# Attention, an ELU layer and a Mish layer on one core: states loaded first on two queues, identity from an iota, four slices and one output weight moved to split form, and new engine times in the plan

## The chip, the cores and the metric

One core of a Trainium2 chip runs the whole program. The metric is the device time of one execution in microseconds (us); lower is better. TensorE (PE) multiplies, VectorE (DVE) and ScalarE (ACT) do the elementwise work, GpSimd (POOL) a few memsets and reductions, and SyncE (SP) issues most of the transfers.

## What is computed

Inputs are float32. `x` is (4, 8, 512, 64), `state` is (4, 8, 32, 64), and each of the two feed-forward layers has `w_in` (512, 2048) and `w_out` (2048, 512). Cut from the reference:

```python
scores = scale * x @ state.T            # tokens read the state
xread  = softmax(scores) @ state        # (4, 8, 512, 64)
scores2 = scale * state @ x.T           # the state reads the tokens
sread  = softmax(scores2) @ x           # (4, 8, 32, 64)
y = concat([xread, sread], axis=2)      # -> (2176, 512) token rows
h = y @ moe_w_in;  y = elu(h) @ moe_w_out
h = y @ moe2_w_in; y = (h * tanh(softplus(h))) @ moe2_w_out
```

In the kernel the weights arrive as 64-bit words and are turned into float32 on the chip, by ScalarE and VectorE.

## The kernel before

**A plan sets every order.** The program first collects operations in a `Plan`: each has one engine or a choice of two (`EITHER`: ScalarE or VectorE), a cost in us, what it reads and writes, and a due time, either given or worked backwards from its successors (`dues`). `run` is a list scheduler: it takes for each engine the operation that can begin first (then the one due first) and emits instructions in that order. On the chip each engine runs its list strictly in order and waits for semaphores; so the costs in the plan affect nothing but orders and the choice between ScalarE and VectorE. The queues SP and ACTQ (transfers issued by ScalarE) are planned with an issue time, a rate and a latency.

**The start.** `load_states(0, 1)` brings the state of batch 0 in two transfers, `load_states(1, B)` the others. `states` transposes them on PE with the identity (L418) and copies them into the block layout `sd`. `front(b, hf)` loads x of batch b, head half hf, in two transfers (`load_x`, L560), transposes it (xT, L681) and multiplies by `sd` into scores (L692); `back` does the softmax on VectorE and ScalarE (L714 to L726), transposes the result (pT, L731) and copies it to the first layer's operand `x1`. `make_ident` (L337 to L346) builds the identity on VectorE. `warm` runs 14 bf16 products on zeroes (L361) ahead of it all; their operand is the zeroed `sd[3]`.

**The first layer** is organised in steps (b, j) over 16 slices of 128 hidden units for each batch of 512 tokens, in the order `FIRST`: slices 0 to 7 of batch 0, 0 to 7 of batch 1, then 8 to 15 of each, then batches 2 and 3. The attention output is never formed: `fold` (L528) multiplies the state into the slice of `w_in` and gives `m`, and a step multiplies `m` by the softmax. `mm1` makes the hidden slice h, `hidden` applies the ELU, `mm2` of the step two back adds g times `w_out` into four accumulators.

**Two forms of a product.** In the split form each float32 operand is a sum of two fp32r parts (hi is a cast, lo a subtraction), and three fp32r products replace the float32 one: L850 to L852 in `mm1`, L950 to L952 in `mm2`. In the whole form the float32 operands go to PE directly: L836 in `mm1` for the steps in `WHOLE` (slices 0 to 7 of batch 0), L938 in `mm2` for the first `WHOLE_OUT` slices of batch 0. Each float32 product leaves two records in the trace. The split form needs more of VectorE and ScalarE: `fold_slice` (cast and L549) for the slice of `m`, `split_first` (cast and subtraction) once for the softmax of batch 0, `split_g` (L914, L915) for g, `split_weight` (cast and L496) for `w_out`.

**After the first layer's start** come the state reads (`state_reads`, `squares` for batches 2 and 3), the conversion of the second layer's weights into a DRAM buffer, four steps for the state rows, and the second layer in five token blocks (L850 to L852, L897 to L915, L950 to L952).

Of the kernel before, what the change touches and what calls it, by code (L numbers as in the profile page):

```python
# [53 lines left out]
class Op:  # L54
    __slots__ = ("engs", "cost", "fn", "preds", "succs", "bufs", "due", "n", "end", "lag", "seq")


class Plan:
# [59 lines left out]
    def run(self, take, dma):  # L118
# [18 lines left out]
        while todo:  # L137
            best = None
            for e, lst in ready.items():
                at = free.get(e, 0.0)  # L140
                cand, first = None, None
                for due, seq, t, op in lst:
                    if op.end is not None:
                        continue
                    ok = True
                    need = {}
                    for b in op.bufs:
                        if b.t is None:
# [12 lines left out]
                    k = (t, due, seq)  # L161
                    if cand is None or k < cand[0]:
# [33 lines left out]
            else:  # L196
                free[e] = op.end = t + c
# [19 lines left out]
def attention_elu_mish(  # L217
# [59 lines left out]
    def act(n):  # L277
        return 0.22 + 0.00075 * n

    def dve(n):  # L280
        return 0.16 + 0.00104 * n
# [53 lines left out]
    def make_ident():  # L335
        cols, rows = (pools["at"].tile([P, 32], F32, tag=n, bufs=1, name=f"ident_{n}") for n in ("col", "tot"))
        nc.vector.memset(cols[:, 0:1], 0.0)  # L337
        w = 1
        while w < 32:
            nc.vector.tensor_scalar(cols[:, w:2 * w], cols[:, 0:w], float(w), None, ALU.add)  # L340
            w *= 2
        nc.vector.transpose(rows, cols)
        nc.vector.memset(ident, 0.0)
        for a in range(4):
            r = slice(32 * a, 32 * (a + 1))
            nc.vector.tensor_tensor(ident[r, r], cols[r, :], rows[r, :], ALU.is_equal)  # L346

    add("DVE", 2.8, make_ident, w=["ident"], due=-50.0)
# [41 lines left out]
    def zero():  # L390
        return sd[B - 1].rearrange("p g h t n -> p (g h t n)")[:, 0:P].bitcast(mybir.dt.bfloat16)
# [5 lines left out]
    def load_states(b0, b1):  # L397
# [13 lines left out]
    def states(b0, b1, due=None):  # L411
# [8 lines left out]
        A("PE", 0.25 * (b1 - b0), turn, r=["ident", (raw, 0), (raw, 1)], w=[pt], due=due)  # L420
        for b in range(b0, b1):
            for i in range(2):
                r = slice(i * D, (i + 1) * D)
                A(EITHER, {"ACT": 0.41, "DVE": 0.43}, lambda e, b=b, i=i, r=r: copy(
# [12 lines left out]
    def weight(kind, layer, j, due=None):  # L437
# [24 lines left out]
        add("ACT", 0.68, lambda: nc.scalar.activation(y.t, words()[0].bitcast(F32), AF.Prelu, scale=2.0 ** -112,  # L462
                                                      alpha=2.0 ** 32), r=[raw], w=[y])

        add("DVE", 0.43, lambda: nc.vector.tensor_scalar(u32(y), u32(y), 3, None, ALU.logical_shift_left), r=[y], w=[y])
# [13 lines left out]
        add("DVE", 0.69, lambda: nc.vector.scalar_tensor_tensor(  # L479
# [12 lines left out]
    def split_weight(kind, layer, j, v):  # L492
        w = w_sb[kind, layer, j] = buf("w", f"w_{kind}", NF, [P, 2, DM], F32R, f"w_{kind}{layer}_{j}_")
        add(EITHER, {"ACT": 0.61, "DVE": 0.43}, lambda e: copy(e, w[:, 0, :], v.t), r=[v], w=[(w, 0)])
        lo, cost = (nc.gpsimd, {"POOL": 1.3}) if (kind, layer, j) in POOL_LO else (nc.vector, {"DVE": 0.69})
# [45 lines left out]
    def fold_slice(s):  # L541
# [6 lines left out]
        add(EITHER, {"ACT": 0.41, "DVE": 0.33}, lambda e: copy(e, t[:, 0], src()), r=keys, w=[(t, 0)])  # L548
        add("DVE", 0.43, lambda: nc.vector.tensor_tensor(t[:, 1], src(), t[:, 0].bitcast(F32), ALU.subtract),  # L549
# [5 lines left out]
    def load_x(b, hf, due=None):  # L555

        t = buf("at", "xb", XB, [P, HH, NC, D], F32, "xb")
        for q in range(2):
            h = hf + 4 * q
            A(SP, 256.0 * (W_WEIGHT if early else 1.0), lambda q=q, h=h: nc.sync.dma_start(  # L560
# [4 lines left out]
    def load_x_ones(b, hf):  # L565

        t = buf("at", "xb", XB, [P, NC, HH, D + 1], F32, "xb1_")
        A("POOL", 0.1, lambda: nc.gpsimd.memset(t[:, :, :, D:], 1.0), w=[(t, HH)])
        for h in range(HH):
# [3 lines left out]
              w=[(t, h)], lag=1.0)  # L573
        return t

    def squares(b):

        xq = []
        for q in range(2):
            t = buf("at", "xb", XB, [P, 2 * S], F32, "xq")  # L580
            xq.append(t)
            for u in range(2):
                for e in range(2):
# [3 lines left out]
                        out=t[r].rearrange("p (k i) -> p k i", i=NS), in_=src), w=[(t, u, e)], lag=1.0)  # L587
# [5 lines left out]
        pr = buf("at", "xb", XB, [P, 2 * S], F32, "prob")  # L593
# [13 lines left out]
        A("PE", TILED + 0.9, score, r=[*xq, ("sd", b, 0), ("sd", b, 1)], w=pts, lag=1.0, place=[raw])  # L607
# [18 lines left out]
        A("DVE", 0.19, lambda: nc.vector.tensor_scalar(mx.t, mx.t, EPS, None, ALU.add), r=[mx], w=[mx])  # L626
        A("DVE", 0.35, lambda: nc.vector.reciprocal(mx.t, mx.t), r=[mx], w=[mx])
# [15 lines left out]
    def front(b, hf):  # L643
# [31 lines left out]
        lag = 0.0 if early else 1.0  # L675
        for q in range(2):
# [8 lines left out]
            A("PE", NC * (0.11), turn, r=["ident", (xb, q)], w=[pt], lag=lag, place=[xT])  # L685
            A(EITHER, both(S), lambda e, q=q, pt=pt: copy(e, xT[:, q, :], pt.t), r=[pt], w=[(xT, q)])
        pt = bank("scores")
        for q in range(2):
            def score(q=q):
                for i in range(4):  # L690
# [5 lines left out]
            A("PE", 0.9, score, r=[(xT, q), ("sd", b, 0), ("sd", b, 1)], w=[(pt, q)], lag=lag, place=held)  # L696
        all_c = [(pt, q) for q in range(2)]
# [5 lines left out]
    def back(b, hf):  # L703
# [10 lines left out]
        A("DVE", 0.69, lambda: nc.vector.tensor_reduce(mx.t, pv(), AX.X, ALU.max), r=all_c, w=[mx])  # L714
        less = A("DVE", 0.69, lambda: nc.vector.tensor_tensor(prg(), pv(), wide(mx), ALU.subtract),
                 r=all_c + [mx], w=[kp])
        A("ACT", 0.64, lambda: nc.scalar.activation(pr(), pr(), AF.Exp, scale=SCALE), r=[kp], w=[kp], lag=lag)
# [5 lines left out]
        A("DVE", 0.69, lambda: nc.vector.tensor_reduce(sm.t, prg(), AX.X, ALU.add), r=[kp], w=[sm])  # L723
        A("DVE", 0.17, lambda: nc.vector.tensor_scalar(sm.t, sm.t, EPS, None, ALU.add), r=[sm], w=[sm])
        A("DVE", 0.25, lambda: nc.vector.reciprocal(sm.t, sm.t), r=[sm], w=[sm])
        A("DVE", 0.69, lambda: nc.vector.tensor_tensor(prg(), prg(), wide(sm), ALU.mult), r=[kp, sm], w=[kp])  # L726
# [15 lines left out]
    def state_reads(b, due):  # L742
        st = buf("at", "own", 1, [P, 2, D])
        den = buf("at", "den", 2, [P, 2])
        xbs, raws = [], []
        order = "(c p f) -> p c f" if b in SQUARES else "(p c f) -> p c f"
        for hf in range(2):
            xbs.append(load_x_ones(b, hf))
# [8 lines left out]
            A("DVE", 1.04, lambda raw=raw, col=col: nc.vector.tensor_reduce(  # L757
# [43 lines left out]
    def split_first():  # L801
# [4 lines left out]
        for hf in range(2):  # L806
            add(EITHER, {"ACT": act(S), "DVE": 0.43}, lambda e, hf=hf: copy(e, t[:, 0, hf, :], v[:, hf, :]),
                r=[(v, hf)], w=[(t, hf, 0)])
            add("DVE", 0.69, lambda hf=hf: nc.vector.tensor_tensor(
# [52 lines left out]
    def hidden(s, h):  # L862
# [3 lines left out]
        if kind < 2:  # L866
# [4 lines left out]
            add("ACT", act(n) + 0.12, lambda: nc.scalar.activation(E(), E(), AF.Relu, bias=one, scale=-1.0),  # L871
# [21 lines left out]
        for q, (c0, c1) in enumerate(g.parts):  # L893
# [4 lines left out]
            add("DVE", 0.1 + 0.00065 * n, lambda c=c: nc.vector.tensor_scalar(e[:, c], e[:, c], E20, None, ALU.min),  # L898
# [3 lines left out]
            add("ACT", act(n) + 0.12, lambda c=c: nc.scalar.activation(e[:, c], u[:, c], AF.Ln, bias=two),  # L902
                r=[ku, "two"], w=[ke])
            add("ACT", act(n) + 0.03, lambda c=c: nc.scalar.activation(e[:, c], e[:, c], AF.Exp, scale=-1.0),  # L904
# [56 lines left out]
    def retire(kind, blk, j, acc, s):  # L961
# [22 lines left out]
        for i, a in enumerate(acc):  # L984
# [29 lines left out]
    def load_x2(nb):  # L1014
# [8 lines left out]
        for k in range(NK):  # L1023
            add(EITHER, {"ACT": act(m * P), "DVE": 0.43},
# [112 lines left out]
WHOLE_J = 8  # L1137
# [6 lines left out]
GATE_READS, GATE_READS_STEP, GATE_SECOND = 10, 8, 14  # L1144
TILED = 0.36
BACKLOG, RATE = 3.0, 330.0
# [7 lines left out]
WHOLE_OUT = 2  # L1154
# [6 lines left out]
WARM, EARLY, XB, EBUFS, GBUFS, FOLD_LAG = 14, 8, 3, 2, 2, 3.0  # L1161
# [25 lines left out]
```

## Time and profile before

| | |
|---|---|
| time, median of 3 runs | 718.62 us (718.62 to 718.7) |
| the profiled execution's own time | 718.71 us |
| its span, first to last instruction | 716.7 us |
| busy: PE, DVE, ACT, POOL | 711.1, 524.0, 418.6, 9.7 us |
| granted TensorE clock over the span | 1.000 |

The span leaves out 2.0 us around the first and the last instruction. Busy time is the union of an engine's instructions; two matmuls in flight overlap, so the mean duration of one is longer than their spacing. In the trace, L12 is line 12 of the kernel, and names such as `sd<-st` are the tile written and the tile read.

### The profile page before, as it was taken

What the parts mean: (1) busy time and instruction counts of PE and PEld (TensorE: products, weight loads), DVE (VectorE), ACT (ScalarE), POOL (GpSimd) and SP (SyncE); (2) the same over time, 40 slices, a digit from 0 to 9 for tenths busy, and PEclk for the clock granted to TensorE, in tenths of its full rate; (3) what the DMA queues carried; (4) which work ended last, traced back from release to release, by engine and by line L of the source; (5) the groups of instructions that cost most, each with busy time, mean ns of one, the idle gap of its engine ahead of it and who ended that gap; (6) DMA issues with size and microseconds to landing.
All of it is one profiled execution on the core that took longest, in us unless ns stands there. A gap on an engine that the chain in (4) does not pass through costs nothing.

```text
span 716.7 us, 10849 instructions
## 1 busy us (share of the span) xinstructions
PE 711.1 (99%) x4070; PEld 587.9 (82%) x4070; DVE 524.0 (73%) x981; ACT 418.6 (58%) x749; POOL 9.7 (1%) x25
## 2 busy tenths in 40 slices
PE   9999999999999999999999999999999999999998
PEld 8467777778777788788888888888999999999996
DVE  7989888887787756887898556665577667556565
ACT  5876766665566744775756445444465545445544
POOL 1000000100000000000000000000000000000000
PEclk9999999999999999999999999999999999999999
DMA  9745879462947765667871003000030011001001
GB/s 311 266 147 161 187 222 219 120 167 66 229 104 222 219 206 151 200 193 217 255 243 50 0 1 103 0 1 1 0 104 1 0 38 51 1 0 45 1 0 45
DMA packets 90039, 81.50 MB, mean 114 GB/s; under 512 B 46468, under 2 KB 69764, under 8 KB 89988
## 3 DMA queue, kind: packets, MB, share of 16 engines
q1 hardware_dynamic: 89300, 80.56, 38.2%
q8 instruction: 32, 0.52, 0.3%
q10 hardware_dynamic: 688, 0.26, 0.1%
q14 instruction: 19, 0.16, 0.1%
HBM read 59.31 MB, written 21.50 MB: 113 GB/s over the span
## 4 chain that ended last, share of the span: by engine, by line
PE 98%; DMA 1%; ACT 0%; DVE 0%; issue 0%; SPq 0%
PE acc_acc L950 17%; PE acc_acc L951 17%; PE acc_acc L952 17%; PE h L850 13%; PE h L851 12%; PE h L852 12%; PE fold L528 2%; PE h L826 2%; PE h L836 2%; PE acc_acc L938 1%; DMA xb<-in_x 1%; PE sr L774 1%; PE acc_att L951 1%; PE acc_att L952 1%; PE acc_att L950 1%; PE scores L692 1%
## 5 line engine op out<-in xcount | busy, mean ns | idle before, releaser
L914 ACT CAST g<-e 128x512 fp32r<-128x512 f32 (+1 forms) x147 | 85.5, 582 | 79.9 <-DVE e L908 39.3
L915 DVE TENSOR_TENSOR g<-e,g 128x512 fp32r<-128x512 f32 (+1 forms) x147 | 94.0, 641 | 29.3 <-ACT g L914 26.8
L852 PE MATMUL h<-x,w_in 128*128 128x384 f32 (+1 forms) x320 | 114.1, 357 | 0.0
L850 PE MATMUL h<-x,w_in 128*128 128x384 f32 (+1 forms) x320 | 114.1, 356 | 0.0
L851 PE MATMUL h<-x,w_in 128*128 128x384 f32 (+1 forms) x320 | 114.0, 356 | 0.0
L952 PE MATMUL acc_acc<-w_out,g 128*128 128x512 f32 x272 | 106.1, 390 | 0.0
L951 PE MATMUL acc_acc<-w_out,g 128*128 128x512 f32 x272 | 106.0, 390 | 0.0
L950 PE MATMUL acc_acc<-w_out,g 128*128 128x512 f32 x272 | 105.8, 389 | 0.0
L950 PE MATMUL acc_acc<-g,w_out 128*128 128x512 f32 x248 | 99.2, 400 | 0.0
L951 PE MATMUL acc_acc<-g,w_out 128*128 128x512 f32 x248 | 96.8, 390 | 0.0
L952 PE MATMUL acc_acc<-g,w_out 128*128 128x512 f32 x248 | 96.6, 390 | 0.0
L897 ACT ACTIVATE e<-h 128x384 f32<-128x384 f32 (+2 forms) x81 | 42.9, 531 | 75.8 <-PE h L852 72.0
L902 ACT ACTIVATE e<-u,two 128x384 f32<-128x384 f32 (+2 forms) x81 | 53.1, 656 | 47.5 <-DVE u L900 47.4
L898 DVE TENSOR_SCALAR e<-e 128x384 f32<-128x384 f32 (+2 forms) x81 | 31.0, 383 | 63.6 <-ACT e L897 63.4
L906 DVE TENSOR_TENSOR u<-u,e 128x384 f32<-128x384 f32 (+2 forms) x81 | 49.0, 605 | 32.6 <-ACT e L904 32.4
L850 PEld LDWEIGHTS h<-x,w_in 128*128 128x128 f32 x320 | 60.1, 188 | 5.5
L851 PEld LDWEIGHTS h<-x,w_in 128*128 128x128 f32 x320 | 60.1, 188 | 5.5
L852 PEld LDWEIGHTS h<-x,w_in 128*128 128x128 f32 x320 | 60.1, 188 | 4.9
L952 PEld LDWEIGHTS acc_acc<-w_out,g 128*128 128x128 f32 x272 | 51.0, 188 | 10.5
L951 PEld LDWEIGHTS acc_acc<-w_out,g 128*128 128x128 f32 x272 | 51.1, 188 | 10.4
L950 PEld LDWEIGHTS acc_acc<-w_out,g 128*128 128x128 f32 x272 | 51.0, 188 | 10.4
L950 PEld LDWEIGHTS acc_acc<-g,w_out 128*128 128x128 f32 x248 | 46.5, 188 | 12.5 <-issue 2.8
(147 smaller groups left out, 1119.5 us busy)
## 6 DMA issues: line engine op xcount, KB each, us to landing
raw_in<-in_moe_w_in SPq DMA_DIRECT2D x32, 512.0 KB, 4.8
raw_out<-in_moe_w_out SPq DMA_DIRECT2D x32, 512.0 KB, 4.8
w2d<-wv SPq DMA_DIRECT2D x32, 256.0 KB, 4.6
x2d<-o SPq DMA_DIRECT2D x16, 256.0 KB, 4.5
xb<-in_x SPq DMA_DIRECT2D x32, 128.0 KB, 4.5
back_in<-w2d SPq DMA_DIRECT2D x16, 256.0 KB, 3.2
back_out<-w2d SPq DMA_DIRECT2D x16, 256.0 KB, 2.9
out<-o SPq DMA_DIRECT2D x14, 256.0 KB, 2.2
```

Source lines behind the costliest of these rows:

```text
L850: nc.tensor.matmul(h[:, :n], lhsT=wh, rhs=xh, start=(k == 0), stop=False)
L851: nc.tensor.matmul(h[:, :n], lhsT=wh, rhs=xl, start=False, stop=False)
L852: nc.tensor.matmul(h[:, :n], lhsT=wl, rhs=xh, start=False, stop=(k == nk - 1))
L897: add("ACT", act(n), lambda c=c: nc.scalar.activation(e[:, c], h[:, c], AF.Exp), r=[h], w=[ke])
L898: add("DVE", 0.1 + 0.00065 * n, lambda c=c: nc.vector.tensor_scalar(e[:, c], e[:, c], E20, None, ALU.min), r=[ke], w=[ke])
L902: add("ACT", act(n) + 0.12, lambda c=c: nc.scalar.activation(e[:, c], u[:, c], AF.Ln, bias=two), r=[ku, "two"], w=[ke])
L906: add("DVE", dve(n), lambda c=c: nc.vector.tensor_tensor(u[:, c], u[:, c], e[:, c], ALU.mult), r=[ku, ke], w=[ku])
L914: add("ACT", act(n) + 0.01, lambda: nc.scalar.copy(g[:, 0, c], e[:, c]), r=r, w=[(g, 0, q)])
L915: add("DVE", dve(n), lambda: nc.vector.tensor_tensor(g[:, 1, c], e[:, c], g[:, 0, c].bitcast(F32), ALU.subtract), r=[*r, (g, 0, q)], w=[(g ...
L950: nc.tensor.matmul(acc.t, lhsT=st[:, 0, :], rhs=mv[:, 0, :], start=fst, stop=False)
L951: nc.tensor.matmul(acc.t, lhsT=st[:, 0, :], rhs=mv[:, 1, :], start=False, stop=False)
L952: nc.tensor.matmul(acc.t, lhsT=st[:, 1, :], rhs=mv[:, 0, :], start=False, stop=lst)
```

## The change

Edits at the start:
- The two transfers of batch 0's state go to SP and to ScalarE's queue, one each, instead of both to ScalarE's; the second half of batch 0's x (both head halves) moves from SP to ScalarE's queue.
- The identity is an iota on GpSimd (column minus row) compared with zero on VectorE.
- The warm-up reads a new zeroed tile `nil` and has 12 products instead of 14.
- The score products of `front` are planned one by one instead of four at a time, and batch 0's get due times of their own.

Edits in the first layer: `WHOLE_J` falls from 8 to 4 and `WHOLE_OUT` from 2 to 1, so that steps 4 to 7 of batch 0 take the split form in `mm1` and step 1 in `mm2`; `split_first` begins at step 3 instead of 4.

Edits in the plan: costs by kind of instruction are lower (`act`, `dve` and the constants), a result is now counted as ready some time after its engine is free (`TAIL`), a margin is added between some engines after 45 us of planned time (`MARGIN`), and before 18 us an engine may take an operation that begins a little later but is due earlier (`LOOK`). The state reads begin at steps 8, 18, 28, 38 instead of 10, 18, 26, 34, and for `squares` batches their x tiles are placed together after the scores.

```diff
@@ Plan.run
-                t = max(t, p.end + (0.0 if p.engs == op.engs else self.LAT))
+                t = max(t, p.end - (TAIL["PE"] if p.at == "PE" and op.engs == ("PE",) else 0.0)
+                        + (MARGIN.get((p.at, op.engs[0]), 0.0) if p.end > MARGIN_FROM else 0.0))
...
+                if cand and e in LOOK and cand[0][0] < LOOK_UNTIL:
+                    (t, due, _), op = cand
+                    c = op.cost[e] if isinstance(op.cost, dict) else op.cost
+                    cand = min((q for q in seen if q[0][0] <= t + LOOK[e][0] * c and q[0][1] < due - LOOK[e][1]),
+                               key=lambda q: (q[0][1], q[0]), default=cand)
...
-                free[e] = op.end = t + c
+                free[e] = t + c
+                op.end = t + c + TAIL.get(e, 0.0)
@@ costs
     def act(n):
-        return 0.22 + 0.00075 * n
+        return 0.125 + 0.00077 * n
     def dve(n):
-        return 0.16 + 0.00104 * n
+        return 0.063 + 0.00105 * n
@@ identity and warm-up
-    add("DVE", 2.8, make_ident, w=["ident"], due=-50.0)
+    nil = pools["at"].tile([P, P], F32, tag="tot", bufs=1, name="nil")
+    add("DVE", 0.2, lambda: nc.vector.memset(nil, 0.0), w=["nil"], due=-80.0)
+    off = pools["at"].tile([P, P], mybir.dt.int32, tag="col", bufs=1, name="off")
+    add("POOL", 0.5, lambda: nc.gpsimd.iota(off, pattern=[[1, P]], base=0, channel_multiplier=-1), w=["off"], due=-70.0)
+    add("DVE", 0.25, lambda: nc.vector.tensor_scalar(ident, off, 0.0, None, ALU.is_equal), r=["off"], w=["ident"],
+        due=-50.0)
...
-        add("PE", 0.215 * WARM, lambda: turns(pt, WARM), r=[("sd", B - 1, 0)], w=[pt], due=-40.0)
+        add("PE", 0.215 * WARM, lambda: turns(pt, WARM), r=["nil"], w=[pt], due=-40.0)
@@ load_states
-            for i in range(2):
-                A(ACTQ, 64.0, lambda i=i: nc.scalar.dma_start(out=raw[:, :, i, :], in_=src), w=[(raw, i)], due=-50.0)
+            for i, (q, eng) in enumerate(((SP, nc.sync), (ACTQ, nc.scalar))):
+                A(q, 64.0, lambda i=i, eng=eng: eng.dma_start(out=raw[:, :, i, :], in_=src), w=[(raw, i)], due=-50.0)
@@ load_x
+            aside = early and not b and q
+            A(ACTQ if aside else SP, 256.0 * (W_WEIGHT if early else 1.0), lambda q=q, h=h, eng=(
+                nc.scalar if aside else nc.sync): eng.dma_start(
@@ front
+        soon = -20.0 + 10.0 * hf if early and not b else None
...
-            A("PE", 0.9, score, r=[(xT, q), ("sd", b, 0), ("sd", b, 1)], w=[(pt, q)], lag=lag, place=held)
+                A("PE", 0.24, score, r=[(xT, q), ("sd", b, 0), ("sd", b, 1)], w=[(pt, q, i)], lag=lag, place=held,
+                  due=soon)
@@ steps and constants
-        begin(min(WHOLE_J, 4), split_first)
+        begin(min(WHOLE_J, 4) - 1, split_first)
...
-            begin(s - 3, fold_slice, s)
+            begin(max(0, s - 3), fold_slice, s)
...
-WHOLE_J = 8
+WHOLE_J = 4
...
-GATE_READS, GATE_READS_STEP, GATE_SECOND = 10, 8, 14
+GATE_READS, GATE_READS_STEP, GATE_SECOND = 8, 10, 14
...
+LOOK = {'ACT': (0.6, 1.0), 'DVE': (0.6, 1.0), 'PE': (0.6, 1.0)}
+LOOK_UNTIL = 18.0
+MARGIN, MARGIN_FROM = {('DVE', 'PE'): 0.4, ('ACT', 'PE'): 0.4, ('SP', 'DVE'): 2.0, ('SP', 'ACT'): 2.0, ('SP', 'PE'): 2.0}, 45.0
+TAIL = {"PE": 0.2, "DVE": 0.12, "ACT": 0.13, "POOL": 0.1}
...
-WHOLE_OUT = 2
+WHOLE_OUT = 1
...
-WARM, EARLY, XB, EBUFS, GBUFS, FOLD_LAG = 14, 8, 3, 2, 2, 3.0
+WARM, EARLY, XB, EBUFS, GBUFS, FOLD_LAG = 12, 8, 3, 2, 2, 3.0
```

## Rows read from the trace of the kernel before

**Rows 1.** Stretches: length, busy PE, PEld, DVE, ACT, POOL (x instructions), clock, DMA, GB/s.

```profile
9.36:22.40 13.04, 12.39 (x131) 9.65 (x129) 12.70 (x26) 11.26 (x25) 0.13 (x1) 1.00 1.07 368
22.40:59.70 37.30, 37.30 (x187) 21.79 (x181) 33.47 (x66) 28.74 (x52) 0.00 (x0) 1.00 0.49 168
59.70:110.00 50.30, 50.30 (x362) 39.54 (x361) 44.19 (x85) 37.04 (x66) 1.67 (x3) 1.00 0.73 197
```

**Rows 2.** Whom PE waited for in the whole span: total us, times, longest.

```profile
PE warm L361 <- DVE ident_col L337: 1.5, 1, 1.5
PE fold L528 <- ACT m L275: 0.6, 1, 0.6
```

**Rows 3.** Chain that ended last, up to 40 us: start us, us, what.

```profile
4.62 0.85 PE xT L681 x4
5.48 0.43 PE st L418 x2
5.90 0.87 PE xT L681 x4
7.20 6.05 DMA xb<-in_x
13.95 0.38 PE fold L528 x16
16.84 0.84 PE scores L692 x8
17.68 0.45 PE pT L731 x4
21.70 0.77 PE fold L528 x16
26.10 3.43 PE acc_acc L938 x8
35.47 1.72 PE h L836 x4
37.19 0.23 PE acc_acc L950
```

**Rows 4.** Instructions in order of time, 0 to 7 us.

```profile
0.73 1.45 POOL L395 MEMSET sd<- 128x512 f32 x3 [0.29 <-POOLq L1172]
0.77 1.01 ACTq L404 DMA_DIRECT2D st_raw<-in_state  x2
0.91 0.48 DVE L395 MEMSET sd<- 128x512 f32 x1 [0.91 <-PEq L1172]
1.46 3.17 PE L361 MATMUL warm<-sd 128*128 128x256 bf16 x14 [1.46 <-DVE ident_col L337]
3.05 0.17 DVE L343 MEMSET ident<- 128x128 f32 x1
3.25 0.77 DVE L346 TENSOR_TENSOR ident<-ident_col,ident_tot 32x32 f32<-32x32 f32 x4
4.42 1.06 PE L681 MATMUL xT<-ident,xb 128*128 128x128 f32 x4
6.00 0.75 ACT L275 COPY sd<-st 64x256 f32<-64x256 f32 x2 [3.99 <-PE st L418]
```

**Rows 5.** Transfers into `st_raw` up to 13 us: time from issue to landing.

```profile
DMA to landing us min/median/max: 3.1/3.8/4.5
```

**Rows 6.** Groups of VectorE's instructions from 9.36 to 59.70 us: busy us, mean ns.

```profile
L275 DVE COPY m<-fold 128x256 f32<-128x256 f32 x4 | 1.6, 418 | 0.8 <-PE fold L528 0.8
L549 DVE TENSOR_TENSOR ms<-m,ms 128x256 fp32r<-128x256 f32 x2 | 0.8, 419 | 0.0
```

**Rows 7.** The same of ScalarE, from 9.36 to 59.70 us.

```profile
L275 ACT CAST x1hl<-x 128x512 fp32r<-128x512 f32 x2 | 1.2, 609 | 0.0
L275 ACT CAST ms<-m 128x256 fp32r<-128x256 f32 x1 | 0.4, 407 | 0.4 <-DVE m L275 0.4
```

**Rows 8.** VectorE's instructions in order of time, 56 to 62 us.

```profile
59.62 1.28 DVE L496 TENSOR_TENSOR w_out<-whole,w_out 128x512 fp32r<-128x512 f32 x2
```

More of the change, by code (lines that the diff above doesn't have):

```diff
@@ L54 @@
 class Op:
-    __slots__ = ("engs", "cost", "fn", "preds", "succs", "bufs", "due", "n", "end", "lag", "seq")
+    __slots__ = ("engs", "cost", "fn", "preds", "succs", "bufs", "due", "n", "end", "lag", "seq", "at")
 class Plan:
@@ L140, in run @@
                 at = free.get(e, 0.0)
-                cand, first = None, None
+                cand, seen = None, []
                 for due, seq, t, op in lst:
@@ L332, in attention_elu_mish @@
     T += [T[-1] + 3.0 * i for i in range(1, 4)]
[L335 to L346, printed above, removed]
-    add("DVE", 2.8, make_ident, w=["ident"], due=-50.0)
+    nil = pools["at"].tile([P, P], F32, tag="tot", bufs=1, name="nil")
[4 more added lines that the diff above has]
+        due=-50.0)
     add("POOL", 0.1, lambda: nc.gpsimd.memset(one, 1.0), w=["one"], due=-50.0)
@@ L390, in zero @@
     def zero():
-        return sd[B - 1].rearrange("p g h t n -> p (g h t n)")[:, 0:P].bitcast(mybir.dt.bfloat16)
+        return nil.bitcast(mybir.dt.bfloat16)
     def clear(b):
@@ L423, in states @@
                 r = slice(i * D, (i + 1) * D)
-                A(EITHER, {"ACT": 0.41, "DVE": 0.43}, lambda e, b=b, i=i, r=r: copy(
+                A(EITHER, {"ACT": 0.38, "DVE": 0.34}, lambda e, b=b, i=i, r=r: copy(
                     e, sd[b][r, :, :, i, :],
@@ L493, in split_weight @@
         w = w_sb[kind, layer, j] = buf("w", f"w_{kind}", NF, [P, 2, DM], F32R, f"w_{kind}{layer}_{j}_")
-        add(EITHER, {"ACT": 0.61, "DVE": 0.43}, lambda e: copy(e, w[:, 0, :], v.t), r=[v], w=[(w, 0)])
-        lo, cost = (nc.gpsimd, {"POOL": 1.3}) if (kind, layer, j) in POOL_LO else (nc.vector, {"DVE": 0.69})
+        add(EITHER, {"ACT": 0.52, "DVE": 0.34}, lambda e: copy(e, w[:, 0, :], v.t), r=[v], w=[(w, 0)])
+        lo, cost = (nc.gpsimd, {"POOL": 1.3}) if (kind, layer, j) in POOL_LO else (nc.vector, {"DVE": 0.605})
         add(next(iter(cost)), cost, lambda: lo.tensor_tensor(
@@ L547, in fold_slice @@
         keys = [(m, j % NC, q) for q in range(2)]
-        add(EITHER, {"ACT": 0.41, "DVE": 0.33}, lambda e: copy(e, t[:, 0], src()), r=keys, w=[(t, 0)])
-        add("DVE", 0.43, lambda: nc.vector.tensor_tensor(t[:, 1], src(), t[:, 0].bitcast(F32), ALU.subtract),
+        add(EITHER, {"ACT": 0.31, "DVE": 0.21}, lambda e: copy(e, t[:, 0], src()), r=keys, w=[(t, 0)])
+        add("DVE", 0.34, lambda: nc.vector.tensor_tensor(t[:, 1], src(), t[:, 0].bitcast(F32), ALU.subtract),
             r=keys + [(t, 0)], w=[(t, 1)], lag=0.5)
@@ L563, in load_x, with load_x_ones @@
         return t
-    def load_x_ones(b, hf):
-        t = buf("at", "xb", XB, [P, NC, HH, D + 1], F32, "xb1_")
-        A("POOL", 0.1, lambda: nc.gpsimd.memset(t[:, :, :, D:], 1.0), w=[(t, HH)])
+    def load_x_ones(b, hf, xbs):
+        t = xbs[hf]
+        A("POOL", 0.1, lambda: nc.gpsimd.memset(t[:, :, :, D:], 1.0), r=[("scored", b)], w=[(t, HH)], place=xbs)
         for h in range(HH):
@@ L572, in load_x_ones @@
                 in_=x[b, 2 * h + hf].rearrange("(c p) d -> p c d" if b in SQUARES else "(p c) d -> p c d", c=NC)),
-              w=[(t, h)], lag=1.0)
-        return t
+              r=[("scored", b)], w=[(t, h)], lag=1.0)
     def squares(b):
[L578 to L581, printed above, removed]
+        xq = [buf("at", "xb", XB, [P, 2 * S], F32, "xq") for q in range(2)]
+        pr = buf("at", "xb", XB, [P, 2 * S], F32, "prob")
+        for q, t in enumerate(xq):
             for u in range(2):
@@ L605, in score @@
                                          start=True, stop=True, tile_position=(u * D, k * NS))
[L607 removed]
+        A("PE", TILED + 0.9, score, r=[*xq, ("sd", b, 0), ("sd", b, 1)], w=[*pts, ("scored", b)], lag=1.0,
+          place=[raw])
         for u in range(2):
@@ L688, in front, with score @@
         for q in range(2):
-            def score(q=q):
-                for i in range(4):
+            for i in range(4):
+                def score(q=q, i=i):
                     h, c = 2 * q + i // 2, i % 2 * 2
@@ L694, in score @@
                         lhsT=xT[:, q, i * P:(i + 1) * P], rhs=sd[b][:, hf, h, :, :], start=True, stop=True)
-            A("PE", 0.9, score, r=[(xT, q), ("sd", b, 0), ("sd", b, 1)], w=[(pt, q)], lag=lag, place=held)
-        all_c = [(pt, q) for q in range(2)]
+                A("PE", 0.24, score, r=[(xT, q), ("sd", b, 0), ("sd", b, 1)], w=[(pt, q, i)], lag=lag, place=held,
+                  due=soon)
+        all_c = [(pt, q, i) for q in range(2) for i in range(4)]
         if ahead:
@@ L744, in state_reads @@
         den = buf("at", "den", 2, [P, 2])
-        xbs, raws = [], []
+        xbs = [buf("at", "xb", XB, [P, NC, HH, D + 1], F32, "xb1_") for hf in range(2)]
+        raws = []
         order = "(c p f) -> p c f" if b in SQUARES else "(p c f) -> p c f"
         for hf in range(2):
-            xbs.append(load_x_ones(b, hf))
+            load_x_ones(b, hf, xbs)
             raw = buf("at", ("scores", "raw")[hf], 1, [P, NC, P])
@@ L806, in split_first @@
         for hf in range(2):
-            add(EITHER, {"ACT": act(S), "DVE": 0.43}, lambda e, hf=hf: copy(e, t[:, 0, hf, :], v[:, hf, :]),
+            add(EITHER, {"ACT": act(S), "DVE": 0.34}, lambda e, hf=hf: copy(e, t[:, 0, hf, :], v[:, hf, :]),
                 r=[(v, hf)], w=[(t, hf, 0)])
-            add("DVE", 0.69, lambda hf=hf: nc.vector.tensor_tensor(
+            add("DVE", 0.605, lambda hf=hf: nc.vector.tensor_tensor(
                 t[:, 1, hf, :], v[:, hf, :], t[:, 0, hf, :].bitcast(F32), ALU.subtract),
@@ L869, in hidden @@
             add("ACT", act(n), lambda: nc.scalar.activation(E(), Hh(), AF.Exp), r=[h], w=[e])
-            add("ACT", act(n) + 0.12, lambda: nc.scalar.activation(E(), E(), AF.Relu, bias=one, scale=-1.0),
+            add("ACT", act(n) + 0.11, lambda: nc.scalar.activation(E(), E(), AF.Relu, bias=one, scale=-1.0),
                 r=[e, "one"], w=[e])
@@ L901, in hidden @@
                 u[:, c], e[:, c], 2.0, e[:, c], ALU.add, ALU.mult), r=[ke], w=[ku], after=sw)
-            add("ACT", act(n) + 0.12, lambda c=c: nc.scalar.activation(e[:, c], u[:, c], AF.Ln, bias=two),
+            add("ACT", act(n) + 0.1, lambda c=c: nc.scalar.activation(e[:, c], u[:, c], AF.Ln, bias=two),
                 r=[ku, "two"], w=[ke])
-            add("ACT", act(n) + 0.03, lambda c=c: nc.scalar.activation(e[:, c], e[:, c], AF.Exp, scale=-1.0),
+            add("ACT", act(n) + 0.02, lambda c=c: nc.scalar.activation(e[:, c], e[:, c], AF.Exp, scale=-1.0),
                 r=[ke], w=[ke])
@@ L913, in split_g @@
         n, c = c1 - c0, slice(c0, c1)
-        add("ACT", act(n) + 0.01, lambda: nc.scalar.copy(g[:, 0, c], e[:, c]), r=r, w=[(g, 0, q)])
+        add("ACT", act(n), lambda: nc.scalar.copy(g[:, 0, c], e[:, c]), r=r, w=[(g, 0, q)])
         add("DVE", dve(n), lambda: nc.vector.tensor_tensor(
@@ L1023, in load_x2 @@
         for k in range(NK):
-            add(EITHER, {"ACT": act(m * P), "DVE": 0.43},
+            add(EITHER, {"ACT": act(m * P), "DVE": 0.34},
                 lambda e, k=k: copy(e, xt[0][:, k, :m * P], raw[:, k, :m * P]), r=[raw], w=[(xt[0], k)])
```

46 lines of the change are left out of this document (23 added, 23 removed).

## The prediction, made before the changed kernel was run

> **What bounds the kernel now.** I read the stretches first, then TensorE's waits, the chain, the first 9 us in order of time, and last the instructions of VectorE and ScalarE up to 60 us.
>
> The stretches show PE busy through both stretches that follow 22.40 us, and before that all but 0.65 us of 9.36:22.40 [rows 1]. The list of PE's waits has two entries in the whole run, 1.5 us before the first warm-up product and 0.6 us before a fold [rows 2]. So the time is PE's own work, plus what it loses in the first 22 us, plus the tail after the last product, which the change leaves alone. A busy PE is not a useful one, though. The reader is to see three losses: 4.42 us before the first real transpose; transposes at half speed, 0.85 us for four of them against 0.45 for four later, which is the ratio of the clock's two levels, 1.2 and 2.4 GHz, though the granted clock of the span is given as 1.000; and restarts after short waits [rows 3, 4].
>
> The second reading is that VectorE is nearly as loaded while the first steps run: from its first maximum at 9.36 to 59.70 us it is busy 12.70 + 33.47 = 46.17 of 50.34 us, ScalarE 11.26 + 28.74 = 40.00 [rows 1]. It hides behind PE by a few us of prepared work, no more.
>
> **Fewer passes of TensorE: -2.0 us.** A step of block 0 kept whole takes four L836 records of 0.43, 1.72 us [rows 3]. With hi and lo halves it takes six products; those of L950 to L952 follow each other at 0.23 [rows 3]: 6 x 0.23 = 1.38. Steps 4 to 7 change form: 4 x 0.34 = 1.36. The second product of step 1 takes eight L938 records in 3.43 us now, and twelve of 0.23 after, 2.76: 0.67. Together 2.0. Step 0 keeps its form. Since PE never idles after 22.40 us, these count in full unless PE is made to wait.
>
> **The start: -0.5 us.** The state loads were issued one behind the other on ScalarE's queue, at 0.77, and landed 3.1 us after issue at best and 3.8 for the second of the pair [rows 4, 5]: about 5.1 us. Issued side by side at 0.75 and alone in front, both land near 3.9. The identity is ready at 4.02 now, after a memset, five additions, a transpose, a memset and four comparisons; then it takes an iota on GpSimd and one comparison. Neither has a row. The iota costs between nothing and the 0.48 us of one of POOL's three 128x512 memsets (1.45 together), the comparison between the 0.17 of VectorE's 128x128 memset and the 0.77 of today's four small ones [rows 4]. From 0.73 on that gives 0.9 to 2.0, and either end is hidden by the loads. The warm-up starts after a 0.17 memset instead of a 0.48 one, at about 1.1 instead of 1.46, and twelve products of 0.21 end near 3.7 against 4.42 [rows 4]. The first transposes can therefore run at 3.9 instead of 4.42: 0.5. From there PE's order is full: four fronts with 32 xT transposes and 32 score products (64 records), and 8 transposes of states, are needed whatever comes first. The x loads on SP move back by one issue (0.5 us), one per half moves to ScalarE's queue; the cover is that PE has the states to transpose first and that ScalarE has nothing until 6.00. Without it x would be late by 0.5 us and the gain is nil. The states copied to sd (ACT, 6.00 to 6.75 now) come about 1 us sooner, and so do the scores' maxima on VectorE; that gives VectorE a head start which I use below.
>
> **The gaps up to 22 us: -0.6 us.** From 4.42 to 22.40 are 18.0 us. Needed at full rate: 48 transposes (8 pT among them) of 0.11 (5.3), 64 scores records at 0.84 for eight (6.7), four L836 records of 0.43 (1.7), two small folds of 0.38 and one of 0.77 (1.5): 15.2 us [rows 3]. Of the 2.8 lost, ten transposes at half speed are 1.1 (the three rows 4.62 to 6.77), the rest, 1.7, are gaps: waits for the last x loads, for VectorE's softmax, and the fold behind ScalarE's m copy. Scores cut into single products, the priority by due time below 18 us and the truer costs touch those. Bounds: nothing and 1.7; the loads that cause two of the gaps stay limited by the transfers (the wait on x ends at 13.25 in the chain), so I take 0.6, nearer the low end.
>
> **VectorE pays: +0.8 us.** The four changed steps need hi and lo slices of m: on VectorE 4 x 0.42 (L549) [rows 6], the casts 4 x 0.41 on ScalarE [rows 7]. Block 0's x must be split at step 3 instead of later: two subtractions of 0.60 (two queued ones take 1.28, each 0.68 long [rows 8]) and two casts that ScalarE runs in this stretch already [rows 7]. Step 1 needs its g split (a subtraction of 0.60 and a cast of 0.61, like those of x1hl) and its w_out subtraction (0.60), one of the two at 59.62 now [rows 7, 8]. Sum 1.7 + 1.2 + 0.6 + 0.6 = 4.1 us on VectorE and about 2.2 on ScalarE, all ahead of block 1's first steps. Both together are 86.2 + 6.3 = 92.5 us, 46.2 each if they were shared evenly. If PE ran the 3.1 us of the terms above ahead, and VectorE began 1 us sooner, the stretch is 48.2 us long: VectorE at 46.2 + 4.1 = 50.3 does not fit; with some 2.5 us of copies moved to ScalarE (the 128x256 copies of m alone are 1.6 [rows 6]) it is 47.8 and fits at 99%. Bounds: no wait at all, if the planner orders it perfectly, and 4.1 us if nothing hides. It sits near its limit, but softmax work of block 1 and conversions wait in front of slack, so I take 0.8.
>
> **At nothing.** The costs in the plan, tails and margins alter only orders; so do the changed start of the state reads and x tiles held for them. Their cover is PE's queue, with no wait after 22.40, and VectorE's spare 6.1 us in 59.70:110.00 [rows 1]. Bounds: a fold or read left waiting costs 0.6 us, as the wait before a fold shows [rows 2]; no gain is possible there, PE being full.
>
> **Sum.** The profiled execution took 718.71, span 716.7 and 2.0 around it. 718.71 - 2.0 - 0.5 - 0.6 + 0.8 = 716.4; the median 718.62 is 0.09 lower, so **716.3**.
>
> **Rivals.**
> *Full recovery.* The gaps close too and VectorE keeps up: 718.62 - 2.0 - 0.5 - 1.7 = 714.4. For: nothing but order stands in the way of it. Against: VectorE's 99%.
> *Eaten.* VectorE costs 2.5 to 3 us instead of 0.8, as the 92% it is busy now may be what such an order reaches: 718.62 - 3.1 + 2.75 = 718.3, no change. For: 4.1 us added where 4.2 were free.
> *Late clock.* Warm-up ends near 3.7, transposes start at 3.9 or later, and full rate comes up to 3 us later: at half rate that loses 1.5 us, so 717.8. For: two products fewer. Against: the wait is short. Now half speed lasts through the three pieces from 4.62 to 6.77 [rows 3]. The Trainium skill, "TensorE: Matmul & The Clock Gate", Part 1 (The HAM clock gate), says that the array starts throttled, that recent activity releases it, and that the point varies from run to run; by that rule a lull after the warm-up could put the rise off, and the time would be this rival's 717.8. The trace of before has no such lull, so it doesn't show it.
> *Slower.* One mechanism: x and m slices of step 4 stand behind conversions in VectorE's in-order queue, and PE's in-order queue stands with them, with the folds and second products behind. If VectorE runs at 92% with nothing moved to ScalarE, 50.3 / 0.92 = 54.7 us from 8.4 end at 63.1 instead of 59.7: PE reaches block 1 3.4 later than now, with every gain already counted in, so 718.62 + 3.4 = 722.0. It decides from 4.5 us of waiting on (3.1 of gain + 1.4). For: the load. Against: ScalarE's 10 us of room.
>
> **How the numbers follow.** Chances: forecast 0.45, full recovery 0.17, eaten 0.18, late clock 0.07, slower 0.13. About 0.2% (1.4 us) is what a measurement can tell from no change: faster is below 717.2, slower above 720.1. Faster: 0.45 + 0.17 + 0.03 of the mixed cases = 0.65; same 0.22; slower 0.13. The range holds full recovery and eaten: 714.3 to 719.0.
>
> **What would show it.** Right: sixteen L836 and eight L938 records; first transposes of st near 3.9; PE waits of at most about 1 us in 22:60, with VectorE over 95% there; L836 of step 1 near 21. Wrong: PE waits of several us on ms, x1hl or w_out between 25 and 60 us (eaten, slower), half-rate transposes beyond 7 us (late clock), or waits of PE past 60 us, which I costed at nothing.

## The result, and the profile after

The change made the kernel slower: 726.9 us (median of five, 726.47 to 730.03) against 718.62, ratio 1.0129 with the interval [1.011, 1.0148]. Forecast were 716.3 and a range from 714.3 to 719.0. The span grew from 716.7 to 724.6 us, all of it in the first 28 us: the first product of step 0's h began at 27.56 us instead of 17.97, and from there on 1.7 us came back, so that the second layer begins 7.9 us late (342.9 against 335.0).

The first row is from the instructions of one line (POOLq is GpSimd's sequencer), the rest are instructions in order of time:

```profile
L347 POOLq MODIFY_POOL_CONFIG  x2: 11/11/11, 0.8 to 0.8; - x2
```

```profile
9.04 0.23 POOL L347 IOTA off<- 128x128 int32 x1 [8.60 <-issue]
9.23 1.44 POOL L396 MEMSET sd<- 128x512 f32 x3
9.30 1.52 DVE L348 TENSOR_SCALAR ident<-off 128x128 f32<-128x128 int32 x1 [7.76 <-POOL off L347]
10.88 0.69 PE L419 MATMUL st<-ident,st_raw 128*128 128x128 f32 x2 [7.09 <-DVE ident L348]
11.37 1.91 PE L683 MATMUL xT<-ident,xb 128*128 128x128 f32 x8
13.30 3.65 PE L694 MATMUL scores<-sd,xT 128*128 128x64 f32 x16
```

The iota takes 0.23 us, but it begins 8.2 us after the change of GpSimd's configuration that its line carries (`MODIFY_POOL_CONFIG`, at 0.8 us). The memsets of `sd` stand behind it in GpSimd's order, and the comparison beside them takes 1.52. The first real product of PE comes at 10.88 instead of 4.42 [rows 4]. Then sixteen scores records need 3.65 us, where eight needed 0.84 [rows 3]. The stretches say why (columns as in [rows 1]):

```profile
7.40:10.90 3.50, 0.01 (x1) 0.02 (x1) 1.52 (x1) 0.00 (x0) 1.71 (x6) 0.51 1.08 361
10.90:20.90 10.00, 9.98 (x47) 9.61 (x47) 4.74 (x9) 2.25 (x5) 0.13 (x1) 0.50 0.63 185
20.90:25.00 4.10, 4.10 (x48) 3.63 (x49) 3.70 (x9) 3.51 (x9) 0.13 (x1) 0.98 1.06 393
25.00:60.00 35.00, 34.94 (x227) 22.80 (x227) 34.60 (x71) 30.57 (x61) 0.00 (x0) 1.00 0.52 176
```

The reader is to see the clock column: after PE had stood idle since the warm-up's end at 3.8 us, the granted clock was 0.50 (1.2 GHz) for the whole of 10.90:20.90. PE is "busy" in 9.98 of these 10 us and gets through 47 products. The last row shows VectorE at 34.60 of 35.00 us. The list of PE's waits in the whole run has two entries:

```profile
PE st L419 <- DVE ident L348: 7.1, 1, 7.1
PE warm L362 <- DVE nil L345: 1.1, 1, 1.1
```

### The profile page after: what moved, and what is told of

Same layout as the page of the kernel before. It is cut to its first block, busy times and chain, and to the rows that moved or that the text cites. A ratio compares the mean times of both kernels' runs of the same rounds, so it can differ in the third digit from the quotient of the medians.

```text
span 724.6 us, 10842 instructions
## 1 busy us (share of the span) xinstructions
PE 712.9 (98%) x4080; PEld 593.5 (82%) x4080; DVE 525.1 (72%) x989; ACT 413.6 (57%) x741; POOL 9.3 (1%) x26
## 4 chain that ended last, share of the span: by engine, by line
PE 98%; DMA 1%; issue 0%; DVE 0%; ACT 0%; ACTq 0%; POOL 0%; POOLq 0%
PE acc_acc L954 17%; PE acc_acc L955 16%; PE acc_acc L956 16%; PE h L854 13%; PE h L855 12%; PE h L856 12%; PE fold L529 2%; PE h L830 2%; PE scores L694 1%; PE h L840 1%; PE xT L683 1%; DMA xb<-in_x 1%; PE sr L778 1%; PE acc_att L955 1%; PE acc_att L954 1%; PE acc_att L956 1%
## 5 line engine op out<-in xcount | busy, mean ns | idle before, releaser
L918 ACT CAST g<-e 128x512 fp32r<-128x512 f32 (+2 forms) x148 | 86.2, 582 | 106.2 <-DVE e L912 47.7
L919 DVE TENSOR_TENSOR g<-e,g 128x512 fp32r<-128x512 f32 (+2 forms) x148 | 94.8, 641 | 38.8 <-ACT g L918 37.8
L954 PE MATMUL acc_acc<-g,w_out 128*128 128x512 f32 x252 | 99.7, 396 | 0.0
L955 PE MATMUL acc_acc<-g,w_out 128*128 128x512 f32 x252 | 98.2, 390 | 0.0
L956 PE MATMUL acc_acc<-g,w_out 128*128 128x512 f32 x252 | 98.1, 389 | 0.0
L954 PEld LDWEIGHTS acc_acc<-w_out,g 128*128 128x128 f32 x272 | 51.0, 188 | 10.4
L955 PEld LDWEIGHTS acc_acc<-w_out,g 128*128 128x128 f32 x272 | 51.1, 188 | 10.4
```

The source lines that it names most:

```text
L918: add("ACT", act(n), lambda: nc.scalar.copy(g[:, 0, c], e[:, c]), r=r, w=[(g, 0, q)])
L919: add("DVE", dve(n), lambda: nc.vector.tensor_tensor(g[:, 1, c], e[:, c], g[:, 0, c].bitcast(F32), ALU.subtract), r=[*r, (g, 0, q)], w=[(g ...
L954: nc.tensor.matmul(acc.t, lhsT=st[:, 0, :], rhs=mv[:, 0, :], start=fst, stop=False)
L955: nc.tensor.matmul(acc.t, lhsT=st[:, 0, :], rhs=mv[:, 1, :], start=False, stop=False)
L956: nc.tensor.matmul(acc.t, lhsT=st[:, 1, :], rhs=mv[:, 0, :], start=False, stop=lst)
```

## The experiments

Each time stands beside runs of the kernel before on the same chip (medians 718.84 to 719.13); the theory is A, that the iota is held up by the change of GpSimd's configuration.

**e1: the identity by the old instructions on VectorE, all else as changed** (the definition of `make_ident` comes back too and is left out here).

```diff
-    nil = pools["at"].tile([P, P], F32, tag="tot", bufs=1, name="nil")
+    nil = pools["at"].tile([P, P], F32, tag="own", bufs=1, name="nil")
-    off = pools["at"].tile([P, P], mybir.dt.int32, tag="col", bufs=1, name="off")
-    add("POOL", 0.5, lambda: nc.gpsimd.iota(off, pattern=[[1, P]], base=0, channel_multiplier=-1), w=["off"], due=-70.0)
-    add("DVE", 0.25, lambda: nc.vector.tensor_scalar(ident, off, 0.0, None, ALU.is_equal), r=["off"], w=["ident"],
-        due=-50.0)
+    add("DVE", 2.8, make_ident, w=["ident"], due=-50.0)
```

> The changed kernel, with the identity made on VectorE by the old fifteen or so instructions (the zeroed tile of the warm-up takes another slot, own). Theory A (GpSimd's iota is held up by the loading of its code, 0.81 to 9.04 us, and everything else of the change works as predicted): the identity is ready by 4 us, the first transposes run at 4, the clock rises near 6.5, and the time is 715 to 717. Rival B (the other parts cost too: VectorE bound between 25 and 60 us, or the new order): 718 to 722. Rival C (the twelve products are too few to hold the clock): half-rate transposes beyond 8 us and about 2 us more than under A.

Measured: median 720.37, ratio 1.0015 [1.0002, 1.0028], and the executions fall apart in groups: five from 718.07 to 718.61, six from 721.15 to 721.92, one at 719.6. So the iota explains most of the loss, but what is left is no gain: A is right about the identity and wrong about 715 to 717. The profile is of the lower group (718.5). From its waits of PE:

```profile
PE scores L704 <- ACT prob L284: 0.9, 1, 0.9
PE scores L704 <- DVE xT L284: 0.7, 2, 0.4
PE xT L693 <- DMA xb<-in_x: 0.6, 1, 0.6
PE h L864 <- DVE e L892: 0.6, 1, 0.6
```

**e2: the iota alone in the kernel before** (the definition of `make_ident` goes).

```diff
-    add("DVE", 2.8, make_ident, w=["ident"], due=-50.0)
+    add("POOL", 0.5, lambda: nc.gpsimd.iota(off, pattern=[[1, P]], base=0, channel_multiplier=-1), w=["off"], due=-70.0)
+    add("DVE", 0.25, lambda: nc.vector.tensor_scalar(ident, off, 0.0, None, ALU.is_equal), r=["off"], w=["ident"],
+        due=-50.0)
```

> The kernel before, with the identity alone made by the iota and one comparison. Theory A: the iota begins near 9 us, the identity is ready near 10.8, the transposes wait 6.4 us for it, the clock falls in that wait and some 4 us more go to half rate: 718.6 + 8 to 11 = 727 to 730. Rival B (the iota is only slow in the new order, and most of the loss is elsewhere): 719 to 723.

Measured: 725.56, ratio 1.0091 [1.0078, 1.0104], 6.6 us more. A holds, at less than its 8 to 11; iota at 8.93, first transposes at 10.78. Half speed lasted less long than in the changed kernel: four transposes took 1.12 us from 10.78, but 0.61 from 14.74.

**e3: an iota that nothing reads, behind GpSimd's memsets.**

```diff
+    off = pools["at"].tile([P, P], mybir.dt.int32, tag="own", bufs=1, name="off")
+    add("POOL", 0.5, lambda: nc.gpsimd.iota(off, pattern=[[1, P]], base=0, channel_multiplier=-1), w=["off"], due=-49.0)
```

> The kernel before, with one more instruction: an iota on GpSimd behind its memsets, which nothing reads. Theory A (the wait is the time from the instruction that changes GpSimd's configuration to the first iota, some 8.2 us, wherever it stands): configuration near 2.2 us, iota near 10.4, time unchanged at 718.6 within 0.3. Rival D (something at the program's start, transfers or a fixed moment, holds GpSimd until about 9 us whatever it does): iota near 9.0, time unchanged too.

Measured: ratio 1.0006 [0.9995, 1.0017], the iota late and free:

```profile
2.15 0.10 POOL L350 MEMSET two<- 128x1 f32 x1
12.42 0.27 POOL L352 IOTA off<- 128x128 int32 x1 [10.17 <-DMA xb<-in_x]
```

GpSimd works until 2.25 us without delay and then stands still for 10.2. D falls: no fixed moment near 9 us holds it. A's 10.4 was missed too, by 2.0 us: the delay follows the instruction, but it isn't a fixed 8.2. The releaser named in the row is an inference; nothing in this kernel makes the iota wait for x.

**e4: 72 warm-up products in the changed kernel.**

```diff
-        add("PE", 0.215 * WARM, lambda: turns(pt, WARM), r=["nil"], w=[pt], due=-40.0)
+        add("PE", 0.215 * WARM, lambda: turns(pt, 72), r=["nil"], w=[pt], due=-40.0)
```

> The changed kernel with 72 warm-up products instead of 12 (the plan still counts 12, so that all orders stay). Theory A splits the loss into the wait (unchanged: first transpose near 10.9) and the clock: with products until about 11 us the clock stays at its upper level, the stretch 10 to 21 us shows 1.00 instead of 0.50, and the time falls by some 4 us, from 726.9 to 722 to 723.5. Rival (the clock costs nothing because VectorE would not have kept up): 726 to 727.

Measured: 724.06, ratio 1.0067 [1.0053, 1.008], by the medians 2.8 us below the changed kernel. The transposes come at 11.63 and run at full rate (first two rows: the chain; third: the stretch, columns as in [rows 1]):

```profile
13.33 1.97 PE scores L694 x16
15.30 0.89 PE xT L683 x8
10.90:20.90 10.00, 9.01 (x92) 8.08 (x90) 7.20 (x14) 4.75 (x11) 0.26 (x2) 1.00 0.63 187
```

So the clock is at least 2.8 of the loss and the wait for the identity most of the rest. More than 2.8 is possible: the identity was ready at 9.95 here, but 72 products were too many and ran until 11.79, so the transposes began 0.75 us later than in the changed kernel. The gain is also held down by VectorE: with PE at full rate the chain runs over VectorE's copies and softmax from 16 to 22 us.

**e5, e6, e9: what the split forms are worth.** e5 is e1 with `WHOLE_J = 8` and `WHOLE_OUT = 2`; e6 is the kernel before with `WHOLE_J = 4`, `WHOLE_OUT = 1` and the split and slices begun earlier as in the change; e9 is e7 (below) with the edit of e5.

```diff
@@ e5, e9
-WHOLE_J = 4
+WHOLE_J = 8
-WHOLE_OUT = 1
+WHOLE_OUT = 2
@@ e6
-        begin(min(WHOLE_J, 4), split_first)
+        begin(min(WHOLE_J, 4) - 1, split_first)
-            begin(s - 3, fold_slice, s)
+            begin(max(0, s - 3), fold_slice, s)
-WHOLE_J = 8
+WHOLE_J = 4
-WHOLE_OUT = 2
+WHOLE_OUT = 1
```

> The kernel with the identity on VectorE (e1), with the old forms: eight whole slices in the first product and two whole output weights. TensorE's nominal work rises by 2.1 us. If the split forms are worth their passes in this order (theory A), about 2 us slower than e1: near 720.3 where e1 took 718.3. Rival B (VectorE gives the passes back, the wait on it at 60 us and the gaps before 20 us): within 0.7 us of e1.

> The kernel before with the split forms alone (four whole slices, one whole output weight, the split of x and the slices begun a step earlier), all costs of the plan, loads, identity and warm-up as before. Theory A (TensorE's passes count in full): 718.9 - 2.0 = 716.9. Rival B (VectorE cannot take 4.1 us more between 9 and 60 us): 718 to 719, with waits of TensorE on VectorE or ScalarE between 25 and 60 us.

> The kernel of e7 (identity on VectorE, 18 warm-up products) with the old forms, eight whole slices and two whole output weights. The profile of e5 had its clock rise at 13.7 us, so e5 against e1 mixes forms and clock; with 18 products the clock should rise before 7 us in every execution. Theory A (in the new order VectorE carries the split forms and the passes count): 718.4 + 2.1 = 720.5. Rival (the passes are given back to VectorE): 718.5 to 719.2.

e5 took 722.38 to 723.98 in all five executions, and its profile had the half rate until 13 us, as the chains of e5 (first row) and e1 (second) show:

```profile
10.88 1.71 PE xT L693 x8
8.91 0.89 PE xT L693 x8
```

So it tells nothing of the forms. (The clock column of e5's profile shows 1.00 in these stretches; here the products' own times show the rate.) e6: 718.9, ratio 0.9999 [0.9991, 1.0008]. B is right about the time: PE waited where it had not,

```profile
PE xT L681 <- DMA xb<-in_x: 1.2, 2, 0.7
PE acc_acc L938 <- ACT sd L275: 0.7, 1, 0.7
PE fold L528 <- DVE m L275: 0.5, 1, 0.5
PE fold L528 <- DVE w L479: 0.4, 1, 0.4
PE acc_acc L951 <- DVE g L915: 0.3, 1, 0.3
```

and gave the passes back. Not all of it is VectorE's and ScalarE's doing: the first entry is two waits on x's loads, at 6.6 and 13.2 us; the other four, 1.9 us, stand against 0.6 in the kernel before [rows 2]. e9: 719.71, ratio 1.0008 [0.9997, 1.0018] against e7's 0.9993 [0.9984, 1.0001], so in the new order the forms are worth about 0.15%, 1.1 us of 2.0, between the theory and its rival. The two intervals together leave room for about 0.1 to 2.0.

**e7: e1 with 18 warm-up products. e8: e1 with the old queues**, both state transfers on ScalarE's, x on SP.

```diff
@@ e7
-        add("PE", 0.215 * WARM, lambda: turns(pt, WARM), r=["nil"], w=[pt], due=-40.0)
+        add("PE", 0.215 * WARM, lambda: turns(pt, 18), r=["nil"], w=[pt], due=-40.0)
@@ e8
-            for i, (q, eng) in enumerate(((SP, nc.sync), (ACTQ, nc.scalar))):
+            for i, (q, eng) in enumerate(((ACTQ, nc.scalar), (ACTQ, nc.scalar))):
-            aside = early and not b and q
+            aside = False
```

> The kernel with the identity on VectorE (e1), with 18 warm-up products instead of 12 (the plan counts 12, orders unchanged). They end near 4.9 instead of 3.8, and the transposes of the states follow; x lands at 5.4 in any case. e1 took 718.1 to 718.6 in half of its executions and 721.2 to 721.9 in most others. If the lull of 12 products (idle 3.8 to 4.1 and 4.8 to 5.4) lets the clock rise later in some executions (theory C), the upper group goes away and the median falls from 720.4 to 718.5. Rival (the two groups come from something else): both groups stay.

> The kernel with the identity on VectorE (e1), with the old loads: both transfers of batch 0's state on ScalarE's queue, all of x on SP. In e1 TensorE waits until 5.41 for x, 0.65 us in all, and starts its transposes of x 1 us later than before. If putting the states ahead of x delays x and with it the start (theory D), the first transposes of x come at 4.1 to 4.4 and the time falls by 0.6 to 1.2 us against e1's lower group, to 717.1 to 717.7. Rival (the start is set elsewhere): 718.3 as e1.

e7: eleven executions from 718.03 to 719.28, the upper group gone; ratio 0.9993 [0.9984, 1.0001]. C holds as far as times show; no execution of the upper group was profiled. e8: 718.54, ratio 1.0005 [0.9994, 1.0015], four of twelve in the upper group again. x's transposes began at 4.07 and it did not help: D, here the loads as what sets the start, falls.

**e10: e7 without the priority by due time. e11: e7 with x's first half ahead of the states and 15 warm-up products. e12: both.**

```diff
@@ e10, e12
-LOOK = {'ACT': (0.6, 1.0), 'DVE': (0.6, 1.0), 'PE': (0.6, 1.0)}
+LOOK = {}
@@ e11, e12: load_x, and turns(pt, 15) for turns(pt, 18)
-                in_=x[b, h:h + 3:2].rearrange("h (p c) d -> p h (c d)", c=NC)), w=[(t, q)], due=due, lag=1.0)
+                in_=x[b, h:h + 3:2].rearrange("h (p c) d -> p h (c d)", c=NC)), w=[(t, q)],
+                due=-60.0 if early and not b and not hf else due, lag=1.0)
```

> The kernel of e7 with the priority by due time below 18 us switched off. Theory E (that priority puts two copies before the first softmax subtraction on VectorE, 10.67 us against 10.08 in the kernel before, and with other orders of the first 20 us gives back 1 us): the first product of h comes before 18.0 us and the time falls below 718. Rival (the priority helps, as it is meant to): the first product of h comes later than 18.1 us and the time rises by 0.5 to 2 us.

> The kernel of e7 with the first half of batch 0's x ahead of the states on both queues, and 15 warm-up products, which end near 4.3. x should land at 4 instead of 5, the transposes of x begin near 4.3. Theory F (the loads' order sets the start): first scores near 6.0 instead of 6.6 and 0.5 to 0.8 us off the time, 717.7. Rival (VectorE's softmax and copies set it): 718.3 to 718.6, as in e8.

> The kernel of e11 (identity on VectorE, 15 warm-up products, x's first half ahead of the states) with the priority below 18 us switched off as in e10. If what the two gave back is separate (e11 took 1.2 us off e7, e10 0.7), 716.6; if both cured the same wait, the one on copies before the softmax's first subtraction, 717.2 as e11.

e10: 717.73, 0.9987 [0.9978, 0.9995]; e11: 717.28, 0.9977 [0.9968, 0.9986]; e12: 717.09, 0.9982 [0.997, 0.9993], with one execution of twelve at 722.11. All three beat both kernels; the three are not told apart by their intervals. e10 came as E said (first product of h at 17.93, time below 718), but its interval overlaps e7's, so E is not settled. e12's median is nearer to 717.2 (one wait cured twice) than to 716.6. In e11 the reason was not the expected one, since its first scores came at 7.90, later than e7's 6.60. What went was waits behind the start: of e7's 0.9 us on ScalarE's copy of prob, 0.7 on xT and 0.6 on e none is in its list.

```profile
PE warm L372 <- DVE nil L345: 1.1, 1, 1.1
PE scores L704 <- ACT sd L284: 0.4, 1, 0.4
```

Which part of the order brought that, the runs don't settle.

**e13: the changed kernel with GpSimd's memsets of `sd` ahead of the iota**, one execution.

```diff
-    add("POOL", 0.5, lambda: nc.gpsimd.iota(off, pattern=[[1, P]], base=0, channel_multiplier=-1), w=["off"], due=-70.0)
+    add("POOL", 0.5, lambda: nc.gpsimd.iota(off, pattern=[[1, P]], base=0, channel_multiplier=-1), w=["off"], due=-56.5)
```

> The changed kernel with GpSimd's three memsets of sd ahead of the iota instead of behind it. If the comparison is slowed by GpSimd's memsets beside it, it takes 0.2 to 0.3 us here; if int32 input makes it slow, 1.5 us again. The configuration changes near 2.2 us instead of 0.81; if the iota follows 8 to 10 us behind it, it begins at 10.4 to 12.4, and the time stays within 1.5 us of the changed kernel's 726.9.

```profile
14.23 0.23 POOL L347 IOTA off<- 128x128 int32 x1 [12.04 <-issue]
14.49 0.23 DVE L348 TENSOR_SCALAR ident<-off 128x128 f32<-128x128 int32 x1 [12.95 <-POOL one L350]
```

The comparison takes 0.23 us without large memsets beside it: they made it 1.52, not int32. The iota came at 14.23, 12.0 us after the memsets, later than the 10.4 to 12.4 expected, and the time, 730.77, is 3.9 above the changed kernel's, beyond the 1.5 expected.

## Why the prediction was wrong

**The step that failed** is in the start: "The iota costs between nothing and the 0.48 us of one of POOL's three 128x512 memsets" and "either end is hidden by the loads". The instruction was inside these bounds (0.23); the time before it was not priced at all. It came out as 8.2 us from the change of configuration to the iota and a wait of PE of 7.1 us for the identity; alone it cost 6.6 us (e2). The trace of before held a hint that the prediction left out: its reductions on GpSimd have the same change of configuration at 12.3 us and their first run only at 78.8, so whatever the change costs was hidden.

```profile
L759 POOL PARTITION_ALL_REDUCE tot<-col x8: 704/718/1597, 78.8 to 211.3; - x8
L759 POOLq MODIFY_POOL_CONFIG  x2: 11/11/11, 12.3 to 12.4; - x2
```

The comparison was out of its bounds too (1.52 against 0.17 to 0.77), by the memsets beside it.

**The late clock** was a rival at 0.07 and 1.5 us. It came as a consequence of the wait, at 2.8 us or more (e4). Without the wait it came too: e5 and e9 differ only in twelve and 18 warm-up products, e5's profile has half rate until 13 us, and the medians are 3.1 us apart (ratios 1.0055 and 1.0008). So the rival's price was half of what the clock cost. By their times, ten of the 24 executions of e1 and e8 (twelve products, in e1 idle times at 3.8 and 4.8 us) went the same way, and none of the 33 of e7, e9 and e10 (18 products). The Trainium skill, "TensorE: Matmul & The Clock Gate", Part 1 (The HAM clock gate), says that activity releases the clock and that the point varies; the traces agree on the second: full rate came some 4 us after PE began again in e2 and some 10 us after in the changed kernel, under nearly unbroken work.

**The start without the iota, forecast -0.5**, did not come. The forecast named the condition, "Without it x would be late by 0.5 us and the gain is nil", and the cover was gone: in e1 the first transposes of x wait until 5.41 us, 1 us later than before, with PE idle for 0.6 of it. In e8 they began at 4.07 and the time was no better.

**The gaps, forecast -0.6**, grew instead, as PE's busy time from 4.42 to 22.40 us shows in the kernel before (first row) and in e7 (second):

```profile
4.42:22.40 17.98, 17.33 (x166) 14.49 (x165) 15.73 (x31) 11.99 (x27) 0.25 (x2) 1.00 1.08 361
4.42:22.40 17.98, 16.39 (x145) 13.08 (x143) 14.32 (x30) 13.76 (x28) 0.25 (x2) 1.00 1.09 362
```

PE was idle for 0.65 us before and for 1.6 in e7. The forecast's 1.7 us of gaps was the remainder of a sum and not an idle time that a row shows; 0.65 us was all there was. The priority below 18 us may be part of the new gaps: without it e10 is 0.06% below e7, within both intervals.

**The passes, -2.0**, are in the trace (sixteen L840 and eight L942 records), and **VectorE's price, +0.8**, agrees with the runs: e9 against e7 leaves about 1.1 of 2.0, so it took about 0.9, with the room of the two intervals. VectorE was as full as forecast, in e1 for the whole of this stretch, and PE never waited in it. It waited just behind it:

```profile
22.40:59.70 37.30, 37.30 (x222) 25.62 (x221) 37.30 (x76) 29.62 (x57) 0.00 (x0) 1.00 0.52 170
65.12 0.50 PE L864 MATMUL h<-x,ms 128*128 128x512 f32 x1 [0.63 <-DVE e L892]
```

This is one of the forecast's own signs of being wrong, "waits of PE past 60 us, which I costed at nothing". e7 and e8 have it too, e10 with 0.4 us; e9, with the old forms, has no such wait, so most of VectorE's price in this order may be this one wait.

With the old plan nothing was left of the 2.0 (e6), as in the rival "eaten", though part of e6's waits were on loads. So the plan's new times, costed **at nothing**, may be what makes the forms worth 1 us. That is only argued: e6 and e7 differ in more than these times, and no run had them alone.

## What to carry to other kernels

The first instruction of a new kind on GpSimd has a price before it that its own duration doesn't show: find the change of configuration in the trace, and put such an instruction where nothing waits for it (here for 12 us). When a start is rearranged, check what PE does between warm-up and first product; here a warm-up that ended a few tenths of a us too early cost 3 us in some executions, and six products more cost nothing that the times show. Passes taken from PE count only as far as the engine that pays for them has room.

## What the runs showed of the hardware

From GpSimd's change of configuration, or the end of what stood before it, to the iota went 7.3 to 8.2 us where it stood first at 0.8 us (e4, e2, the changed kernel), and 10.2 to 12.0 where it followed the memsets at 2.2 (e3, e13). What passes in this time, and why it varies, no row shows, and it wasn't tried without the transfers that run beside it. That the change of configuration itself is what holds the iota is likewise not shown: every first iota here had one before it.

A 128x128 comparison on VectorE took 1.52 us beside three GpSimd memsets and 0.23 without (e13), and it ended just behind the last of the three (10.82 against 10.67). The Trainium skill, "SBUF — State Buffer" (SBUF: two separate sides), says that VectorE and GpSimd share a pair of ports, as a lock that the loser waits for, when VectorE's instruction is in a 2-port mode or has two inputs in SBUF (the second only against a GpSimd instruction that reads SBUF). The two durations would fit that, but no row tells the comparison's mode, and one lock for each instruction doesn't say why it waited for all three. Not every instruction of VectorE is held up: its memset of 128x512 took 0.48 us beside GpSimd's memsets in the kernel before [rows 4] and 0.48 without them in the changed one.
